# RWKV attention and a SoLU layer on one core: loads from three queues, and turning by DMA instead of by TensorE

## The chip, the cores and the metric

The kernel runs on one core of one Trainium2 chip. The metric is the device time of one execution in microseconds (us). The engines of the core work side by side, each through its own list of instructions in order: PE (TensorE, the matmuls), DVE (VectorE), ACT (ScalarE), POOL (GpSimd) and SP (SyncE, which computes nothing here and issues transfers). Transfers between the main memory and the on-chip memory, and within the latter, are carried out by 16 DMA engines; an engine that issues one goes on while it runs.

## The reference

Two layers follow each other. The first is a linear attention with a decaying state, for 4 batches, 8 heads, 768 steps and a head size of 48:

```python
for t in range(S):
    cur = np.einsum('bhd,bhe->bhde', u[None] * kt, vt)
    y[:, :, t] = np.einsum('bhd,bhde->bhe', rt, state + cur)
    state = wt[:, :, :, None] * state + np.einsum('bhd,bhe->bhde', kt, vt)
```

Its result, 3072 rows (batch and step) of 384 numbers (head and element), goes through the second:

```python
h = x @ w_in                                   # 384 -> 1024
sm = softmax(h);  solu = h * sm
ln = (solu - mean(solu)) / sqrt(var(solu) + 1e-06) * g_ln
out = ln @ w_out                               # 1024 -> 384
```

Inputs and outputs are float32; r, k, v and w are 4.7 MB each, w_in and w_out 1.6 MB each, the result 4.7 MB.

## The kernel before, in words

The sequence is cut into 6 chunks of 128 steps. A **unit** is one chunk of one batch, 128 rows: 24 units, numbered 0 to 23, four (one per batch) to a chunk. A unit needs four loads, the r, k, v and w of its 128 steps for all heads; each is 192 KB, in 1024 pieces of 48 floats (192 bytes).

What is done for a unit is written as short **words**, and ORDER (line 21) is the list of all words in the order in which they are recorded: a letter name, the unit's number, and after a dot an engine (a = ACT, d = DVE, p = POOL, g = POOL's queue) or the PSUM bank that PE writes. Every engine runs its instructions in the order of the words; the class InOrder (line 72, whose call at line 86 records nearly every instruction, so that nearly all of the profile carries line 86) pins it. Engines wait for each other only where data or a buffer demands it. The order was written out ahead; nothing is scheduled afterwards.

The words of a unit, in the order in which its data flows:

- LW, LK, LR, LV: its four loads, all issued by SP before the change. Each lands in one of 7 buffers (NIO) that units take in turn, so unit i+7 loads only after unit i has been read.
- lw: logarithm of w (ACT). cum: two matmuls that sum the logarithms over time (PE). ex: exponential of both (ACT). kp: k and r scaled by them (DVE), 128 x 1024 in bf16, the heads padded to 64.
- krk, krr: k and r turned, so that the head's elements lie on the partitions: four 128 x 128 transposes each on PE. kr: that result copied out of PSUM (ACT or DVE).
- M: eight small matmuls, the scores. m: scores copied out, masked at once (DVE) or afterwards by sel (POOL).
- p, q, qh, dg, dv: the diagonal term with u (POOL and DVE). vb: v in bf16.
- S, et, st: the state after the chunk, in two buffers per batch. Y, y: the attention's result, 128 x 384.
- X, xT: y turned by three transposes on PE, and copied out (ACT or DVE).
- H: the hidden layer, h with the 1024 features on partitions, 24 matmuls. e: exponential (ACT). he: h times it (DVE). ea: the two halves of e added (POOL), in some units. hq: he squared (ACT or DVE).
- Oa, Ob: he times the prepared w_out (eight matmuls of 385 columns). Matmuls of one column in between sum e (or ea) and hq for the normalisation.
- sq, qm, lv, o, out: the variance, its root, the scaled result, and its store.

The weights come in by LI (w_in, three loads of 512 KB) and LO (w_out, two of 768 KB), are cast or scaled by wi, gw, mn, mc and ce. H of the first unit needs all of w_in. The words hot.. are matmuls on zeros that keep TensorE's clock up while it would idle early on.

In the built program a transfer issued by SP waits on one of eight counters taken in turn, so it is issued only when the transfer eight places before it has landed.

Of the kernel before, what the change touches and what calls it, by code (L numbers as in the profile page):

```python
# [8 lines left out]
F32 = mybir.dt.float32  # L9
# [11 lines left out]
ORDER = """  # L21
LW2 LU0 ik0 lw2 hot5.4 cum2.0 LW1 lw1 us0.7 ih0 LW3 lw3 cum3.2 LR2 uc0 ex2 LK2 p2 LV2 vb2.p kp2 hot4.4 krk2.6 krr2
LR1 LK1 cum1.4 LW0 ex1 kp1 kr2.d hot1.0 S2.7 lw0 et2 LV1 vb1.d LW4 st2 p1 q1 hot2.0 krk1.1 krr1 q2 qh2 dg2 LG0
kr1.a M2.4 ex3 hot1.0 M1.6 m1.d dv2 LR0 LK0 p0 q0 cum0.0 ex0 lw4 cum4.6 ex4 kp0 krk0.1 krr0 LR3 gs0.0 gc0 dg1
m2.d Y2.i0 kr0.d LK3 p3 LR4 LV0 vb0.a dg0 dv1 kp3 Y1.i5 hot3.1 krk3.4 krr3 LK4 kp4 M0.2 m0.d krk4.1 y1.a X1.5
krr4 y2.a X2.0 dv0 xT2.d hot1.6 Y0.n7 y0.d kr3.a M3.2 hot1.0 X0.6 S1.4 p4 q3 kr4.a xT1.a xT0.a LI2 LI1 wi1.a
M4.0 m4.a et1 LI0 S0.5 et0 wi0.d m3.d LO1 wi2.p H1.6 e1 gw5.a H2.0 e2 H0.2 LO0 gw2.a q4 qh4 dg4 qh3 dg3 gw4.p
gw7.p LV3 vb3.p dv3 sel4 LW6 e0 gw6.d st1 LV4 vb4.p he1 lw6 dv4 gw1.d LW5 gw0.d gw3.d mn0.4 mc0 ce5.p ce6.p
Y3.i7 ce4.p he2 st0 he0 cum6.0 y3.a ce7.p hot1.5 X3.6 lw5 xT3.a ce3.d LK6 LR6 p6 Y4.n5 LR5 LK5 ce2.d hq0.a ex6
LW7 cum5.2 H3.6 p5 y4.d ex5 ce1.d ce0.d Oa0.5 kp6 krk6.1 krr6 S4.0 hq1.d Oa1.4 kp5 krk5.3 krr5 X4.2 Ob1 e3 he3  # L30
LV5 q6 q5 kr5.d hq2.a et4 st4 M5.6 kr6.a M6.0 xT4.d lw7 cum7.2 hq3.a sq1 m6.a m5.d dg5 vb5.d qm1 dv5 Ob0 ex7 sq0
qm0 S3.7 qh6 LR7 LK7 p7 kp7 et3 lv1 st3 lv0 H4.0 Y5.n6 y5.d LR9 LK8 o1.d e4 krk7.3 krr7 Oa2.2 he4 X5.7 q7 kr7.d
LW9 lw9 o0.a LK9 p9 LW8 lw8 S5.6 et5 cum9.4 ex9 Ob2 sq2 LR8 p8 st5 dg6 kp9 qm2 LV6 xT5.a LV9 vb6.p dv6 sel6
cum8.0 ex8 kp8 hq4.a LV7 LV11 out1 LW10 dg7 vb7.p dv7 Oa3.3 vb9.a lv2 H5.6 e5 M7.4 m7.d he5 q8 krk9.1 LK10 krr9
kr9.a S9.0 et9 Ob3 sq3 st9 q9 qm3 o2.a out0 ea5.p Y6.i5 y6.a LV8 LR10 Y7.n4 y7.d LW11 LW12 krk8.1 M9.6 lw10 lv3
X6.2 xT6.a m9.d o3.a krr8 LV10 out3 out2 kr8.d qh9 dg9 dg8 hq5.d cum10.4 ex10 kp10 S6.0 vb11.d et6 X7.2 xT7.a
st6 p10 vb8.d dv8 dv9 H6.6 e6 he6 H7.2 lw11 e7 he7 M8.4 m8.a Oa5.1 Y9.n0 Ob5 sq5 y9.d cum11.6 ex11 krk10.5 krr10
qm5 kr10.d S7.4 et7 st7 Oa4.3 hq6.d lv5 lw12 o5.a X9.2 sel8 Y8.i0 vb10.p y8.a LK11 LR11 kp11 xT9.d q10 dg10 p11
M10.4 m10.a sel10 S10.1 et10 st10 dv10 S8.0 et8 S11.7 et11 X8.6 xT8.a LK12 LW13 cum12.4 q11 ex12 lw13 st11 st8
Ob4 sq4 qm4 LW14 LR12 kp12 p12 lw14 lv4 o4.a out5 LK13 LV12 LR13 Y10.n2 dg11 y10.d H8.6 e8 krk12.1 krk11.0 krr11  # L40
krr12 kr12.d he8 kr11.a q12 qh12 cum13.4 H9.2 vb12.p S12.1 ex13 p13 q13 ea7.p dg12 kp13 dv11 LW16 LR14 LK14 e9
he9 et12 st12 M12.6 m12.a Oa6.0 X10.5 xT10.a krk13.4 krr13 kr13.a M11.6 m11.d ea8.p dv12 sel12 p14 cum14.2 ex14
q14 out4 Ob6 sq6 hq8.d M13.4 m13.d LV13 hq7.a LW15 lw15 lw16 kp14 vb13.d H10.6 dg13 qm6 LW18 lw18 Y11.n1 y11.d
Oa8.5 LK16 LR15 LR16 LK15 e10 he10 hq9.a krk14.4 Y12.i3 krr14 lv6 qh14 kr14.d p15 ea10.p dv13 LR18 LV14 vb14.p
q15 qh15 LK18 p18 Ob8 sq8 qm8 y12.a S13.2 et13 st13 o6.a lv8 X11.1 xT11.d cum16.6 ex16 X12.3 hq10.d LW19 kp16
Oa9.4 cum15.0 xT12.a Ob9 ex15 kp15 sq9 o8.a dg14 dv14 qm9 M14.2 m14.a sel14 krk16.7 Oa7.6 krr16 kr16.d lv9 o9.d
cum18.0 ex18 kp18 Ob7 LV15 S14.5 et14 st14 krk15.3 krr15 kr15.d LK19 Y13.i2 lw19 cum19.0 krk18.7 p16 q16 vb15.a
S15.4 y13.a sq7 qm7 dg15 X13.5 xT13.d ex19 LR19 kp19 lv7 o7.a q18 krr18 kr18.d H11.2 et15 st15 krk19.5 krr19
kr19.d LW17 lw17 cum17.0 e11 he11 ex17 ea11.p out8 LK17 LR17 p17 kp17 H12.6 e12 he12 hq11.a p19 H13.4 e13 Oa10.3
Y14.n2 M16.0 m16.a dg16 q19 dv15 y14.d ea12.p ea13.p M15.6 m15.d he13 Ob10 sq10 X14.2 out9 Oa11.1 LW20 qm10 lw20  # L50
cum20.6 hq12.d krk17.0 krr17 out6 out7 LV16 vb16.a dv16 xT14.a S16.2 LR20 ex20 LK20 dg18 et16 st16 lv10 o10.a
H14.4 e14 kp20 Ob11 sq11 kr17.d LK23 qm11 lv11 o11.a Oa12.2 krk20.3 krr20 kr20.a he14 sel16 Y16.n7 y16.d Y15.n6
y15.d M19.4 m19.a M18.0 m18.d Ob12 X15.7 xT15.a q17 hq13.d LV19 LW21 LV17 X16.3 xT16.a ea14.p vb19.a M17.4 m17.d
sq12 LK22 out10 qm12 dg17 qh19 vb17.p sel19 p20 hq14.a LW22 LV20 q20 qh20 dv17 M20.0 LV21 m20.d out11 LK21 H15.6
e15 he15 lw22 ea15.p H16.4 LV18 vb18.p dv18 LR21 p21 lw21 Oa14.3 Y17.n1 LR22 LV23 q21 dg19 dv19 Ob14 LR23 p23
p22 e16 he16 lv12 Oa13.0 LW23 o12.a out12 sq14 qm14 hq15.d vb20.a lv14 dg20 dv20 y17.d cum21.6 ex21 Ob13 cum22.4
sq13 ex22 LV22 vb22.p ea16.p o14.d out14 Y18.n2 y18.d Oa15.1 X18.3 qm13 kp22 lv13 xT18.d X17.2 xT17.a kp21 Ob15
sq15 qm15 S18.5 et18 st18 Y19.n4 y19.d lv15 o15.a out15 o13.a krk22.2 S17.3 et17 lw23 H18.6 e18 ea18.p hq16.d
vb21.d st17 Y20.n5 y20.d X19.4 xT19.d krr22 kr22.a H17.0 he18 hq18.d cum23.4 ex23 kp23 Oa16.3 e17 ea17.p he17
krk21.2 krr21 kr21.a H19.6 e19 krk23.5 X20.4 krr23 q22 qh21 vb23.p out13 xT20.a kr23.a he19 Oa18.2 Ob16 sq16  # L60
M21.0 q23 ea19.p qh23 dg22 dv22 m21.a sel21 qm16 lv16 M22.6 hq19.a M23.4 Ob18 sq18 dg21 H20.0 o16.a out16 m22.d
m23.d Oa19.7 Y22.n6 qm18 lv18 hq17.d Ob19 S19.5 dg23 dv23 e20 Oa17.4 y22.d X22.3 he20 et19 st19 xT22.d dv21
Y21.n6 Ob17 y21.d sq19 o18.a sq17 qm17 lv17 Y23.n1 out18 qm19 lv19 X21.0 xT21.d H22.2 o17.a e22 out17 ea20.p
y23.d H21.0 X23.5 xT23.a e21 hq20.d o19.d out19 Oa20.6 he22 hq22.d H23.4 e23 he21 hq21.d Ob20 sq20 qm20 lv20
o20.a out20 ea22.p Oa22.7 ea21.p Oa21.3 he23 hq23.d Ob22 sq22 qm22 lv22 Ob21 sq21 qm21 lv21 o21.d o22.a out22
out21 ea23.p Oa23.2 Ob23 sq23 qm23 lv23 o23.a out23
"""

NIO, NLW, NKP, NWK = 7, 10, 6, 4


class InOrder:


    def __init__(self, tc, engine):
        self.tc, self.engine, self.last = tc, engine, None

    def __getattr__(self, name):
        make = getattr(self.engine, name)

        def call(*args, **kwargs):
            if self.last is None:
                made = make(*args, **kwargs)
            else:
                with self.tc.issue_after(self.last):
                    made = make(*args, **kwargs)  # L86
            self.last = made.ins
            return made

        return call  # L90
# [3 lines left out]
def kernel(  # L94
# [25 lines left out]
    pe, act, dve, pool, sp = (InOrder(tc, e) for e in (nc.tensor, nc.scalar, nc.vector, nc.gpsimd, nc.sync))  # L120
# [34 lines left out]
    g_rows = consts.tile([KF, 128], F32)  # L155

# [57 lines left out]
    qm_t = ring("qm", NWK, [C, 1], F32)  # L214
    lv_t = ring("lv", NWK, [C, 1], F32)
    rs_t = ring("rs", NWK, [C, 1], F32)

    u_bc = consts.tile([C, H, D], BF16)
# [27 lines left out]
    def load_w(i, x):  # L246
        sp.dma_start(out=w_t[i % NIO][:, :, :D], in_=rows_of(w, i))

    def load_k(i, x):
        sp.dma_start(out=kr_t[i % NIO][:, 0, :, :D], in_=rows_of(k, i))  # L250

    def load_r(i, x):
        sp.dma_start(out=kr_t[i % NIO][:, 1, :, :D], in_=rows_of(r, i))

    def load_v(i, x):
        sp.dma_start(out=v_t[i % NIO][:, :, :D], in_=rows_of(v, i))

    def load_u(i, x):
        sp.dma_start(out=u_row, in_=u.rearrange("(o h) d -> o (h d)", o=1))

    def load_g(i, x):
        sp.dma_start(out=g_rows, in_=moe_g_ln.rearrange("(ko ki) -> ko ki", ki=128))

    def load_w_in(j, x):
        sp.dma_start(out=win_f[:, j, :], in_=moe_w_in[j * 128:(j + 1) * 128, :])

    def load_w_out(j, x):
        part = slice(j * KF // 2, (j + 1) * KF // 2)
        sp.dma_start(out=wout_f[:, part, :],
                     in_=moe_w_out.rearrange("(ko ki) d -> ki ko d", ki=128)[:, part, :])  # L270
# [109 lines left out]

    def scores(i, x):
# [86 lines left out]

    def hidden(i, x):
        xT = xT_t[i % NWK]  # L470
        h_ps = live[i]["h_ps"] = bank([128, KF, C], F32, x, "h_ps")
# [4 lines left out]

    def hidden_exp(i, x):
        act.activation(out=e_t[i % NWK], in_=live[i]["h_ps"], func=EXP)
# [7 lines left out]
    def hidden_mul(i, x):  # L486
        dve.tensor_mul(out=he_t[i % NWK], in0=live[i]["h_ps"], in1=e_t[i % NWK])
# [96 lines left out]
```

## Time and profile before

| What | before |
|---|---|
| time, median of 3 runs | 155.79 us (155.73 to 155.89) |
| the profiled execution's span, first to last instruction | 152.4 us |
| busy: PE, DVE, ACT, POOL | 136.4, 131.8, 120.0, 119.0 us |
| TensorE's mean granted clock | 0.975 |
| transfers | 104825 packets, 27.06 MB |

The profile is of one execution. Its span runs from the first instruction to the last; the time of a run also holds what lies around them, here 3.4 us (155.8 - 152.4). Busy times are sums over the span. Matmuls overlap each other, and the ends given for them are modelled, so the distance from one start to the next tells what a matmul costs. The strip in 40 slices shows each engine's busy share in tenths, and under "DMA" that of the 16 DMA engines.

### The profile page before, as it was taken

What the parts mean: (1) busy time and instruction counts of PE and PEld (TensorE: products, weight loads), DVE (VectorE), ACT (ScalarE), POOL (GpSimd) and SP (SyncE); (2) the same over time, 40 slices, a digit from 0 to 9 for tenths busy, and PEclk for the clock granted to TensorE, in tenths of its full rate; (3) what the DMA queues carried; (4) which work ended last, traced back from release to release, by engine and by line L of the source; (5) the groups of instructions that cost most, each with busy time, mean ns of one, the idle gap of its engine ahead of it and who ended that gap; (6) DMA issues with size and microseconds to landing.
All of it is one profiled execution on the core that took longest, in us unless ns stands there. A gap on an engine that the chain in (4) does not pass through costs nothing.

```text
span 152.4 us, 5172 instructions
## 1 busy us (share of the span) xinstructions
PE 136.4 (90%) x2093; PEld 105.5 (69%) x2093; DVE 131.8 (87%) x227; ACT 120.0 (79%) x247; POOL 119.0 (78%) x149
## 2 busy tenths in 40 slices
PE   6777598968999999999998999999799999999970
PEld 1242365936778889779776689887686988889740
DVE  5029968899999999998999999999999999988940
ACT  4526648869888999799998889998988789938661
POOL 7268986799909994899999997799889979973600
PEclk9959969999999999999999999999999999999998
DMA  3999999989979999989897989995998110112023
GB/s 76 218 216 211 217 334 377 254 175 223 216 151 216 220 204 229 206 177 224 194 203 144 228 195 275 199 199 136 241 205 210 63 45 4 44 63 103 4 79 127
DMA packets 104825, 27.06 MB, mean 178 GB/s; under 512 B 100314, under 2 KB 104419, under 8 KB 104803
## 3 DMA queue, kind: packets, MB, share of 16 engines
q1 hardware_dynamic: 104802, 26.75, 77.4%
q8 instruction: 16, 0.26, 0.7%
q14 instruction: 7, 0.05, 0.1%
HBM read 22.03 MB, written 4.72 MB: 176 GB/s over the span
## 4 chain that ended last, share of the span: by engine, by line
PE 53%; DVE 23%; SPq 8%; ACT 6%; issue 3%; DMA 2%; POOL 1%; DVEq 0%; POOLq 0%
PE ps L86 53%; SPq L86 7%; DVE he L86 6%; DVE m L86 4%; DVE kp L86 4%; DVE w L86 3%; DMA kr_in<-in_k_dram 2%; DVE kr L86 1%; DVE hq L86 1%; DVE y L86 1%; DVE st L86 1%; ACT ps L86 1%; ACT o L86 1%; DVE dg L86 1%; ACT win_sb L86 1%
## 5 line engine op out<-in xcount | busy, mean ns | idle before, releaser
L86 PE MATMUL ps<-w,he 128*128 128x385 bf16 x192 | 44.5, 325 | 1.0 <-DVE w L86 0.7
L86 PE MATMUL ps<-xT,win_sb 128*128 128x128 bf16 x576 | 35.5, 219 | 1.1 <-DVE qm L86 0.8
L86 PEld LDWEIGHTS <-win_sb 128*128 128x128 bf16 x576 | 32.8, 98 | 2.2 <-DVE m L86 0.9
L86 PE MATMUL ps<-one_col,hq 128*128 128x1 bf16 x192 | 31.5, 164 | 0.0
L86 DVE TENSOR_TENSOR he<-ps,e 128x1024 bf16<-128x1024 f32 x24 | 29.1, 1214 | 1.6 <-ACT e L86 1.6
L86 DVE TENSOR_TENSOR kp<-ps,kr_in 128x768 bf16<-128x768 f32 x24 | 22.8, 951 | 7.7 <-DMA kr_in<-in_k_dram 4.9
L86 POOL TENSOR_TENSOR p<-kr_in 128x384 bf16<-128x384 f32 x24 | 24.7, 1038 | 4.5 <-DMA kr_in<-in_k_dram 4.2
L86 POOL TENSOR_TENSOR dv<-vb,dg 128x384 bf16<-128x384 bf16 x24 | 21.7, 907 | 7.5 <-DVE qm L86 3.6
L86 ACT ACTIVATE e<-ps 128x1024 bf16<-128x1024 f32 x24 | 24.5, 1021 | 3.1 <-PE ps L86 2.0
L86 POOL TENSOR_TENSOR ea<-e 128x512 bf16<-128x512 bf16 x17 | 20.0, 1181 | 6.4 <-ACT e L86 5.7
L86 POOL TENSOR_TENSOR q<-p,u_bc 128x384 bf16<-128x384 bf16 x24 | 22.2, 931 | 2.4 <-DVE dg L86 1.7
L86 ACT ACTIVATE ps<-ps 128x768 f32<-128x768 f32 x24 | 19.1, 799 | 5.1 <-PE ps L86 4.3
L86 PEld LDWEIGHTS <-kp 128*128 128x128 bf16 x272 | 17.5, 100 | 6.0 <-DVE kp L86 3.2
L86 PEld LDWEIGHTS <-he 128*128 128x128 bf16 x192 | 18.4, 96 | 4.0
L86 PEld LDWEIGHTS <-hq 128*128 128x128 bf16 x192 | 15.4, 96 | 8.3
L86 DVE TENSOR_TENSOR m<-ps,keep 128x1024 bf16<-128x1024 f32 x15 | 18.2, 1216 | 1.2 <-PE ps L86 1.0
L86 PE MATMUL ps<-ident,kp 128*128 128x128 bf16 x192 | 16.5, 227 | 1.6 <-POOL p L86 1.1
L86 DVE TENSOR_TENSOR hq<-he 128x1024 bf16<-128x1024 bf16 x15 | 13.4, 890 | 0.1
L86 ACT COPY kr<-ps 128x1024 bf16<-128x1024 bf16 x11 | 11.1, 1012 | 2.4 <-PE ps L86 2.4
L86 ACT ACTIVATE lw<-w_in 128x384 bf16<-128x384 f32 x23 | 11.7, 523 | 1.3 <-DMA w_in<-in_w_dram 1.3
L86 PEld LDWEIGHTS <-kr 64*128 64x128 bf16 (+1 forms) x272 | 10.2, 95 | 3.1 <-ACT kr L86 0.7
L86 PE MATMUL ps<-inv_col,ea 128*128 128x1 bf16 x68 | 11.2, 165 | 0.0
(90 smaller groups left out, 293.7 us busy)
## 6 DMA issues: line engine op xcount, KB each, us to landing
w_in<-in_w_dram SPq DMA_DIRECT2D x24, 192.0 KB, 3.7
kr_in<-in_r_dram SPq DMA_DIRECT2D x24, 192.0 KB, 3.7
kr_in<-in_k_dram SPq DMA_DIRECT2D x24, 192.0 KB, 3.7
v_in<-in_v_dram SPq DMA_DIRECT2D x24, 192.0 KB, 3.6
out_dram<-o SPq DMA_DIRECT2D x24, 192.0 KB, 2.6
win_f<-in_moe_w_in_dram SPq DMA_DIRECT2D x3, 512.0 KB, 6.4
wout_f<-in_moe_w_out_dram SPq DMA_DIRECT2D x2, 768.0 KB, 9.0
u_row<-in_u_dram SPq DMA_DIRECT2D x1, 1.5 KB
```

Source lines behind the costliest of these rows:

```text
L86: made = make(*args, **kwargs)
```

## The change

- Loads may be issued by SP, by ACT's queue (".a") or by POOL's (".g"): of the 96 loads of units, 44 stay on SP, 37 go to ACT and 15 to POOL; two of the three loads of w_in go to ACT. Stores stay on SP.
- For units 12 to 23 the words krk, krr, kr and X, xT are gone. In their place stand kt and xt: SP issues a transfer that reads kp (or y) in on-chip memory, turns it on the way, and writes the turned tile.
- For seven units (14, 16, 17, 18, 19, 21, 22) h is computed with rows on partitions (six matmuls of 512 columns instead of 24 of 128). The exponential and the square then give their sums over the features as they are computed (ACT's accumulated output), so that the one-column matmuls and ea fall away; he is turned by a third kind of transfer, ht, before Oa.
- The last unit's hidden layer is done in two halves (HA, EA, DA, QA and HB, EB, DB, QB).
- All other squares are ACT's; DVE squares only the last unit's halves. ea is kept in 9 units instead of 17.
- Transfers of SP and ACT are recorded as one sequence in the order of the words; the eight counters are shared by the two.
- The order is new throughout. Loads and attention of more units come ahead of the weights: in the new order 43 loads of units stand ahead of the last load of w_in (20 before).
- Code for a third way to square (g_ps, below) is there, but no unit uses it.

```diff
 ORDER = """
...
+LW0 LW1.a LR0 LU0 LK0.a LV1 LW3.a lw0 LR1 hot10.0 cum0.4 LV3.g LV5.g lw1 cum1.0 ih0 LK1.a ex0 us0.2 ik0 ex1 p0 kp0
...
+Y2.i5 kp7 cum8.1 kp9 krk7.6 LW10 y2.a vb8.a kr6.d q5 gs0.7 p7 dv4 krr7 X2.3 q6 Y3.i4 LO0 LW11 ex8 S7.0 gc0 LV9.g
+LI0.a kr7.d M7.5 wi1.p kp8 M5.1 krk8.7 y3.a X3.4 xT2.d m7.d gw6.a krr8 Y4.i3 M6.5 xT3.d S6.4 kr8.d gw4.a LK10.a
+m5.a LR10.a krk9.1 S8.7 m6.d gw5.a dg5 wi2.p gw7.a et7 lw10 y4.a krr9 wi0.p LW14 st7 kr9.d sel5 LR14.a et8 LR11
+cum10.5 st8 et6 H0.2 LW17 LW12 st6 H1.0 dv5 LK12 vb9.p ex10 LK14.a e0 kp10 dg6 Y5.i4 gw0.p gw2.p gw3.a he0 H3.5 q7
...
+LK18.a hq5.a Oa4.3 X9.4 he7 out2 LR19.a Ob4 dv10 kt13 he6 dg11 xT9.d p15 sq4 X8.6 Y10.n5 S12.7 et12 hq6.a y10.d qm4
+xT8.d st12 Oa5.2 M14.0 p14 M11.4 vb15.p vb13.p lv4 rs4 m11.a m14.d o4.d kt12 Ob5 ea7.p ea6.p sq5 qm5 lw18 LK20 lw19
...
+M18.2 ea12.p m18.d LK21.a e13 Ob10 sq10 qm10 LW23 S15.0 lw21 lv10 Y15.n6 dg17 et15 y15.d rs10 dv17 xt14 p18 H14.2
...
+HA23.0 Ob19 ht21 hq20.a he22 out18 HB23.3 sv21 ht22 sq19 qm19 Oa20.7 EA23 lv19 DA23 rs19 hq21.a sv22 Oa21.4 o19.d
...
-    pe, act, dve, pool, sp = (InOrder(tc, e) for e in (nc.tensor, nc.scalar, nc.vector, nc.gpsimd, nc.sync))
+    pe, act, dve, pool, sp = (InOrder(tc, e, e in (nc.scalar, nc.sync))
+                              for e in (nc.tensor, nc.scalar, nc.vector, nc.gpsimd, nc.sync))
+    queue = {"": sp, "a": act, "g": pool}
...
     def load_w(i, x):
-        sp.dma_start(out=w_t[i % NIO][:, :, :D], in_=rows_of(w, i))
+        queue[x].dma_start(out=w_t[i % NIO][:, :, :D], in_=rows_of(w, i))
...
+    def turned_kr(i, x):
+        sp.dma_start_transpose(out=kr_s[i % NKP], in_=kp_t[i % NKP].rearrange("t a h d -> t (a h d)"))
+
+    def turned_x(i, x):
+        sp.dma_start_transpose(out=xT_t[i % NWK], in_=y_t[i % NWK])
+
+    def turned_he(i, x):
+        sp.dma_start_transpose(out=he_t[i % NWK], in_=ht_t[i % NHT])
...
     def hidden(i, x):
         xT = xT_t[i % NWK]
+        if i in by_rows:
+            h_ps = live[i]["h_ps"] = bank([C, 2, 512], F32, x, "h_ps")
+            for j in range(KM):
+                for n in range(2):
+                    pe.matmul(h_ps[:, n, :], lhsT=xT[:, j, :], rhs=win_sb[:, j, n * 512:(n + 1) * 512],
+                              start=(j == 0), stop=(j == KM - 1))
+            return
...
+            act.activation(out=flat(e_t[i % NWK]), in_=flat(live[i]["h_ps"]), func=EXP, accum_out=be_t[i % NWK])
...
+            dve.tensor_mul(out=ht_t[i % NHT], in0=flat(live[i]["h_ps"]), in1=flat(e_t[i % NWK]))
...
+            act.activation(out=flat(hq), in_=ht_t[i % NHT], func=SQUARE, accum_out=s2_t[i % NWK])
...
+            if i in by_rows:
+                pe.matmul(o_ps[:, :DM + 1], lhsT=he[:, f, :], rhs=w2[:, f, :], start=(f == 0), stop=(f == KF - 1))
+                continue
...
+                pe.matmul(L["g_ps"], lhsT=he[:, f, :], rhs=he[:, f, :], start=(f == 0), stop=(f == KF - 1))
```

## The prediction

> **What bounds the kernel now.** First the strip of 40 slices, for where each engine is full:
>
> ```profile
> PE   6777598968999999999998999999799999999970
> DVE  5029968899999999998999999999999999988940
> ...
> DMA  3999999989979999989897989995998110112023
> GB/s 76 218 216 211 217 334 377 254 175 223 216 151 216 220 204 229 206 177 224 194 203 144 228 195 275 199 199 136 241 205 210 63 45 4 44 63 103 4 79 127
> ```
>
> PE is full from slice 12 (43 us) to the end; the DMA engines are full from slice 2 to 31 (4 to 118 us) and nearly idle after. Then the chain of work that ended last, in order of time, and PE's own waits, longest first:
>
> ```profile
> 43.27 31.86 PE ps L86 x551
> ...
> 110.34 37.23 PE ps L86 x601
> ...
> 148.56 0.58 ACT o L86
> ...
> PE ps L86 <- DVE w L86: 2.1, 3, 0.9
> PE ps L86 <- ACT lw L86: 2.1, 2, 1.4
> ```
>
> No wait of PE is over 1.4 us, and the last 37 us before the closing scalar steps are PE without a gap. So what sets the end is when PE can start in earnest (43 us) and how much work is then left; and the start is set by loads. For the prices, PE's timeline (start, length, instruction: the distance of the starts is the cost) and the transfers between 76 and 87 us, where SP issues loads alone:
>
> ```profile
> 119.83 1.50 PE L86 MATMUL ps<-xT,win_sb 128*128 128x128 bf16 x24
> 121.17 0.33 PE L86 MATMUL ps<-st,kr 128*128 128x96 bf16 x4
> 121.34 0.36 PE L86 MATMUL ps<-vb,m 128*128 128x48 bf16 x8
> 121.55 0.33 PE L86 MATMUL ps<-ident,y 128*128 128x128 bf16 x3
> 121.72 0.39 PE L86 MATMUL ps<-ident,kp 128*128 128x128 bf16 x4
> ...
> 124.56 0.61 PE L86 MATMUL ps<-ident,kp 128*128 128x128 bf16 x8
> 125.01 1.50 PE L86 MATMUL ps<-xT,win_sb 128*128 128x128 bf16 x24
> ```
>
> ```profile
> DMA packets 10922, 2.08 MB, mean 189 GB/s; under 512 B 10921, under 2 KB 10921, under 8 KB 10921
> ...
> q1 hardware_dynamic: 10921, 2.07, 96.5%
> ```
>
> 96.5% of 16 engines for 11 us over 10921 packets is 15.6 ns a packet; a load, 64 packets on each engine, is 1.0 us of all 16. The five weight loads (3.15 MB) at the 377 GB/s of slice 7 are 8.4 us. From 126 to 146 us only stores run: share 0.14, 52 GB/s, so 0.53 us a store. 96 x 0.995 + 8.4 + 24 x 0.53 = 116.6 us; the page's 77.4% of 152.4 is 118.0.
>
> **PE.** From the starts: 24 hidden matmuls 1.34 us, eight transposes 0.45, three 0.17, half an output with ea 0.81 (123.75 to 124.56), one matmul of 385 columns 0.165. Turning by DMA takes 12 x (0.45 + 0.17) = 7.4 us off PE. A unit by rows has eight matmuls of 385 columns, 1.32 instead of 1.62; its six of 512 columns are, by their columns, 6 x 0.22 = 1.32 instead of 1.34: 7 x 0.32 = 2.2 us. Four more warm-ups (0.86) lie in the early idle time. Summed so over all words PE goes from 125.4 to 116.5 us. As a check: before, the words from cum of unit 7 (43.6 us) on sum to 100.4 us and PE ended at 147.6, 104.0 later; I scale what is left by 1.036.
>
> **The other engines**, by the rows of the costliest groups (busy, mean ns of one), of which three:
>
> ```profile
> L86 DVE TENSOR_TENSOR hq<-he 128x1024 bf16<-128x1024 bf16 x15 | 13.4, 890 | 0.1
> ...
> L86 ACT COPY kr<-ps 128x1024 bf16<-128x1024 bf16 x11 | 11.1, 1012 | 2.4 <-PE ps L86 2.4
> ...
> L86 ACT ACTIVATE hq<-he 128x1024 bf16<-128x1024 bf16 x9 | 9.5, 1055 | 0.5 <-DVE he L86 0.5
> ...
> SPq L86 <- ACT o L86: 22.2, 9, 5.1
> ```
>
> The last line is SP's longest wait, used below. DVE loses 15 squares (13.4), six vb (3.8), weights (3.7), three kr (2.0), gains ten o (6.1), three m (3.7), one y (0.6), 1.4 for sums over unhalved q, 1.1 for halves: 131.8 to 121.8. ACT gains 14 squares (14.8), vb (2.0), w (2.4), seven small squares (1.2), loses nine kr (9.1), twelve xT (5.8), ten o (5.8), three m, one y and a cast (4.5): 120.0 to 115.2. The sums over features have no row: not below nothing, as no element is dropped, and at most one rs (0.2) each, 14 x 0.2 = 2.8; I take 0. ACT's queue also issues 39 loads. SP's issue of a lone load takes 0.37 to 0.43 us, one right behind another 0.87 (median of k's): 14 to 34 us; ACT's stand three us apart, nearest to the lone ones, so 17, and ACT 132. POOL loses eight ea, three sel, seven qh, gains two vb and two casts (-13.6, to 105.4) and issues 15 loads, each between SP's lone 0.37 and its longest, 4.1; nearest to neither, as POOL shows none: 1.0 taken, sum 120. None passes the 150 us of the paths below. The last unit in halves: before, PE has no gap at the end, so I give it 0 (between -0.7, half a hidden layer overlapped, and +0.9 for one more exponential and product in line).
>
> **The transfers.** A turn of kp or he reads 1024 rows of 256 bytes. The nearest row is a load of 1024 packets of 192 bytes; 64 more bytes at 377 GB/s over 16 engines are 2.7 ns, so 18.3 ns a packet, 1.16 us. xt, 384 rows: 0.44. Low end: 256 KB at 377 GB/s, 0.70. High end: nothing overlaps and each holds the engines for a load's median flight, 3.7. Taken: 1.16, and 19 x 1.16 + 12 x 0.44 = 27 us more on engines that are full until 118 us. Every turn waits on SP for its source (kp from DVE for kt, y for xt, the product for ht), and behind it on SP stand loads of units 18 to 23 and the stores; eight places on, the shared counters make ACT wait too, with its exponentials behind (LR22 on ACT waits for kt16's place, LK23 for kt17's).
>
> **The sum.** Transfers in word order, first packet at 2.2 us:
> - To LI0, the last of w_in: 43 loads, 8.4 of weights: 53.4 us (before: 20 loads; DVE's cast began at 25.2). One cast on POOL, 1.0, then H of unit 0, from which PE has 94.7 x 1.036 = 98.1 left: PE ends at 152.5. Half of the nine POOL loads ahead may be overtaken (4.5): 148.0.
> - To kt12: 75 loads, 8.4, four stores, three turns: 90.8; from M12 PE has 62.0 x 1.036 = 64.2 left: 155.0. xt14 (90 loads, ten stores, seven kt, three xt: 114.9; 40.2 left): 155.1. Seven others are in flight, so up to 7 us can be overtaken; half is 3.5: 151.5.
>
> The later one holds: PE ends at 151.5 instead of 147.6. Behind PE's end the old trace has 4.8 us of scalar steps and store, and 3.4 lie around the span: 159.7, say **159.5 us** against the 155.79 median. What goes out of PE (8.9 us) is lost in the start (H of unit 0 some 25 us later) and to the fuller DMA engines. This case's own range: all seven overtaken 156.2, none 163.3.
>
> **Rivals.**
> - *Faster: no DMA idle time.* In the strip of 76 to 87 us slices of 250 to 260 GB/s stand beside some of 9 to 75, and SP waits 22.2 us for ACT's o ahead of stores. Loads on ACT's and POOL's queues don't stand behind stores. At 225 GB/s a load is 0.87: LI0 at 48.0, PE's end 147.1, with half the overtaking (3.9) 143.2; kt12 at 81.5, 145.7, less 3.0 is 142.7. Time 151.4. It decides once PE ends before 147.6, from loads of 0.94 on. Against it: full slices already stand at 9, and at the start, where only loads run, the window from 4 to 24 us has share 1.05.
>  The Trainium skill ("DMA: Bandwidth & Descriptors", "Issuing engines are not separate DMA queues") says that transfers of all issuers run on the same 16 engines and interleave, and that several issuers save only the time to issue; by it a load stays at 1.0 and this rival gains only what is idle. The trace agrees so far as one queue fills all 16.
> - *Slower: ACT becomes the bound.* With 0.87 an issue, ACT's sum is 115.2 + 34 = 149.1; ACT idles 6.1 us of the last 12.4 and about 3 of the first 10, which gives 158.3, time 161.7, up to 165 with waits on counters. For: ACT was busy 9.97 of 10 us from 70 to 80. Against: its issues stand apart.
> - *Much slower: dear turns.* At twice the load's packet time, 2.3 us, xt23 (all loads, 18 stores, 17 large turns and 12 small ones) comes at 165.1 and PE ends 8.3 later: time 181.6; at 3.7 us each, 211. For: no row shows a turn. Against: same rows, same bytes.
>  By the Trainium skill ("VectorE: DVE Perf Modes", "The three transpose paths") a block of 128 x 128 takes 1309 ns by DMA and 390 on TensorE. An estimate by it, 188 blocks one after another, is 246 us, beyond 250 us in all; TensorE's here cost 56 ns, so that such single figures hold mostly fixed time.
> - *The gain and the loss cancel:* PE's end within 0.3 us of 147.6.
>
> **Chances.** Main case 0.42, idle time gone 0.32, ACT 0.13, dear turns 0.09, cancelling 0.04. 0.2% (0.3 us) is about what a measurement of this kernel can tell from no change. Faster: 0.32 and 0.01 of the main case's rim: 0.33; same 0.04; slower 0.63. The range goes from 149 (a good part of the faster case, about 0.1 below) to 170 (ACT's case inside, dear turns out).
>
> **What would show it.** Right: H of unit 0 starting at 48 to 54 us; DMA at 9 until about 130 us; PE with gaps before M12, H14 or H16 whose releaser is a DMA; PE's transposes down to 96 + 36. Wrong: a load's packets clearly under 15 ns or slices above 240 GB/s throughout (faster), ACT-issued loads of 0.8 us or more (ACT), turns landing after more than 6 us (dear), or PE without waits and H of unit 0 before 46 us.

## The result, and the profile after

The changed kernel takes **160.71 us** (median of 4 runs, 159.66 to 161.41) against 155.76 us (4 runs) of the kernel before: a ratio of 1.034, 95% interval 1.028 to 1.040. It is slower, as forecast (159.5 us). Its profiled execution took 161.41 us with a span of 159.7. Some executions of a kernel take over 1.5% longer than its fastest one; the times and ratios of the experiments leave these out.

The strip of the changed kernel in 40 slices of 4 us (busy tenths; GB/s moved):

```profile
PE   6868548979496899999839999968997799999970
...
PEclk9999985799969789999995999999999789999999
DMA  5999999999999569499997998999899967388432
GB/s 106 290 275 256 290 290 256 258 401 380 280 231 200 108 143 206 134 216 186 224 258 222 189 129 192 261 201 190 195 172 201 244 137 181 99 130 221 123 140 101
```

Three things are to be seen. The loads ahead of the weights move at 256 to 290 GB/s, where the kernel before had 211 to 218. The DMA engines are full through slice 31 (128 us; before 118), but for slices 13, 14, 16 and 21 (52, 56, 64 and 84 us). And PE, which was busy 9 tenths and more in nearly every slice from 43 us on, now has holes: slices 10, 12, 20, 26 and 30 to 31 (40, 48, 80, 104 and 120 us). In or after all but that at 104 us the granted clock drops to 0.5 to 0.7.

Where PE waited, from its timeline after the first H (start, length, instruction; in brackets the idle time just before it and what ended it):

```profile
42.49 4.44 PE L86 MATMUL ps<-xT,win_sb 128*128 128x128 bf16 x48 [2.28 <-POOL win_sb L86]
...
52.52 0.33 PE L86 MATMUL ps<-st,kr 128*128 128x96 bf16 x4 [1.91 <-DVE kr L86]
...
84.05 0.40 PE L86 MATMUL ps<-kr 64*128 64x128 bf16 x8 [2.65 <-DMA kr<-kp]
84.38 2.73 PE L86 MATMUL ps<-xT,win_sb 128*128 128x128 bf16 x24
...
87.93 1.50 PE L86 MATMUL ps<-xT,win_sb 128*128 128x128 bf16 x24
...
106.45 1.51 PE L86 MATMUL ps<-xT,win_sb 128*128 128x128 bf16 x24 [1.28 <-DMA xT<-y]
...
111.19 1.47 PE L86 MATMUL ps<-win_sb,xT 128*128 128x512 bf16 x5 [0.37 <-DMA xT<-y]
...
124.94 0.39 PE L86 MATMUL ps<-win_sb,xT 128*128 128x512 bf16 x1 [0.97 <-DMA xT<-y]
```

The lines with a wait are H of unit 0 (42.5 us), Y of unit 6, whose bank still held kr of unit 10, and then M12, H13, H14 and H16: from M12 on it is a turned tile that comes last, but for one wait of 0.97 us on ACT's et at 123.3 us. The two lines without a wait are the same 24 hidden matmuls: right behind the hole of 2.65 us they took 2.73 us, 3.5 us later 1.50. The chain of work that ended last says the same; before, its DMA share was 2% and PE's 53%:

```profile
DMA 33%; PE 26%; ACT 13%; POOL 9%; issue 7%; DVE 7%; SPq 3%; ACTq 0%; POOLq 0%
```

Its pieces in order of time (start, length, what) show which transfers:

```profile
75.67 8.34 DMA kr<-kp
...
84.05 3.07 PE ps L86 x32
...
106.39 4.75 DMA xT<-y
...
111.63 7.01 PE ps L86 x100
...
119.38 5.52 DMA xT<-y
```

The turn in front of M12 took 8.3 us from issue to landing, 3.9 of which SP spent on issuing it. The medians, from the page's DMA issues (how many, us to landing):

```profile
kr<-kp SPq DMA_TRANSPOSE x12, 5.2
xT<-y SPq DMA_TRANSPOSE x12, 2.8
he<-win_f SPq DMA_TRANSPOSE x7, 2.8
```

### The profile page after: what moved, and what is told of

Its sections match the earlier page's. It is cut to its first block, busy times and chain, and to the rows that moved or that the text cites. A ratio compares the mean times of both kernels' runs of the same rounds, so it can differ in the third digit from the quotient of the medians.

```text
span 159.7 us, 4569 instructions
## 1 busy us (share of the span) xinstructions
PE 133.9 (84%) x1750; PEld 96.4 (60%) x1758; DVE 124.5 (78%) x215; ACT 116.3 (73%) x255; POOL 115.1 (72%) x150
## 3 DMA queue, kind: packets, MB, share of 16 engines
q10 hardware_dynamic: 38768, 8.33, 27.6%
## 4 chain that ended last, share of the span: by engine, by line
DMA 33%; PE 26%; ACT 13%; POOL 9%; issue 7%; DVE 7%; SPq 3%; ACTq 0%; POOLq 0%
PE ps L86 26%; DMA xT<-y 6%; DMA w_in<-in_w_dram 6%; DMA kr<-kp 5%; DMA win_f<-in_moe_w_in_dram 5%; DMA kr_in<-in_k_dram 4%; ACT hq L86 3%; DMA v_in<-in_v_dram 3%; SPq L86 3%; ACT e L86 3%; DMA kr_in<-in_r_dram 3%; POOL q L86 2%; DVE kp L86 2%; POOL ea L86 2%; POOL p L86 1%
## 5 line engine op out<-in xcount | busy, mean ns | idle before, releaser
L86 ACT ACTIVATE e<-ps 128x1024 bf16<-128x1024 f32 (+1 forms) x25 | 24.6, 986 | 11.9 <-PE ps L86 10.6
L86 PE MATMUL ps<-xT,win_sb 128*128 128x128 bf16 x408 | 29.0, 236 | 3.6 <-POOL win_sb L86 2.3
L86 PEld LDWEIGHTS <-win_sb 128*128 128x128 bf16 x408 | 26.6, 106 | 5.2 <-POOL win_sb L86 2.7
L86 PE MATMUL ps<-one_col,hq 128*128 128x1 bf16 x136 | 22.3, 164 | 0.6 <-ACT hq L86 0.5
L86 DVE TENSOR_TENSOR he<-ps,e 128x1024 bf16<-128x1024 f32 (+1 forms) x18 | 20.7, 1157 | 1.6 <-ACT e L86 1.6
L86 ACT ACTIVATE hq<-he 128x1024 bf16<-128x1024 bf16 x16 | 16.6, 1052 | 2.5 <-issue 1.3
L86 POOL DMA_DIRECT2D v_in<-in_v_dram x15 | 14.1, 938 | 0.0
L86 POOL TENSOR_TENSOR ea<-e 128x512 bf16<-128x512 bf16 x9 | 10.3, 1154 | 4.5 <-ACT sq L86 3.0
L86 PE MATMUL ps<-kr 64*128 64x128 bf16 x192 | 9.8, 229 | 4.1 <-DMA kr<-kp 2.6
L86 DVE TENSOR_TENSOR y<-ps,dv 128x384 bf16<-128x384 f32 x18 | 9.8, 552 | 3.6 <-POOL q L86 2.2
```

## The experiments

Twelve kernels ran. Ratios are to the kernel before on the same chip, each with its 95% interval. "PE's end" is the start of PE's last matmul in the profile (before 147.4, changed 154.7), "first H" the start of H of the first unit (before 26.1, changed 42.5). In the four runs below that keep the changed kernel up to its first H, this lies at 40.9 to 42.6 us; so a difference of less than 2 us in it says nothing.

### One queue for all loads

```diff
-LW0 LW1.a LR0 LU0 LK0.a LV1 LW3.a ... LV3.g LV5.g
+LW0 LW1 LR0 LU0 LK0 LV1 LW3 ... LV3 LV5
```

> The new kernel with all loads issued by SP again, in the same order of words; turns stay on SP. If several queues let the DMA engines carry more (278 to 290 GB/s in the first 25 us of the new kernel against 211 to 218 before), H of unit 0 comes at 50 to 54 us instead of 42.5 and the time is 168 to 175. If the queues change nothing but the issuing (my prediction's premise), H of unit 0 stays near 43 and the time at 160 to 162; if issuing on ACT and POOL is itself the cost, it falls below 158.

Measured: 175.3 us (two executions), ratio 1.132 (1.125 to 1.140), just above the 168 to 175 us forecast. First H at **54.2 us**, PE's end 168.0. The strip of this kernel:

```profile
DMA  5999999998999899939999999999689996747552
GB/s 112 212 207 192 202 205 220 211 213 211 375 272 264 160 224 183 202 92 230 205 205 163 220 176 182 235 172 216 136 187 154 251 194 135 195 110 177 135 169 91
```

The full engines of one queue move 192 to 220 GB/s ahead of the weights, those of three 256 to 290. The shares say the same: 1.05 with one queue (4 to 36 us, 207 GB/s), 1.23 with three (4 to 32 us, 274 GB/s). The start moves by 11.7 us of the 13.3 by which PE's end moves. So packets of several queues do pass beside each other here, and within the new order the three queues are worth some 15 us (1.132 against 1.034).

### POOL's loads on ACT

```diff
-LV3.g LV5.g ... LV2.g ... LV16.a
+LV3.a LV5.a ... LV2.a ... LV16.a
```

> The changed kernel with its 15 loads on POOL's queue issued by ACT instead, at the same words. Theory (POOL's issuing, 15 x 0.94 = 14 us, stands in front of POOL's own work, on which the attention's dv and the masks wait): first H near 42, POOL's waits shrink, 156 to 159 us. Rival (the third queue's packets pass beside the others, and POOL isn't what is waited for): ACT gets 15 x 0.43 = 6.5 us more, the head's slices fall below 260 GB/s, 162 to 168 us.

Measured: 162.05 us, ratio 1.048 (1.042 to 1.054), against 1.034 (1.028 to 1.040) of the changed kernel. First H at 47.0 us, slices of 235 to 262 GB/s from 4 to 32 us, at a share of 1.24. The rival holds, at its lower edge: POOL's 14 us of issuing are not what is waited for, and the third queue brings the first H from 47.0 to 42.5 us. One queue, two, three: 54.2, 47.0, 42.5. Whether the last step is the third queue or the larger packets in which POOL's loads move (3072 bytes instead of 192) was not tried.

### Nothing turned by DMA

The changed kernel with the words of old for k, r and y, and the seven units no longer by rows (in place of each turn, for instance unit 14's):

```diff
-kt14
+krk14.0 krr14 kr14.d
-xt14
+X14.7 xT14.d
-sv14 ... ht14
```

> The new order and the loads from three queues, but nothing is turned by DMA: kt, xt and ht are taken out, krk, krr, kr (copied by DVE), X and xT (DVE) stand in their places, and the seven units by rows go the old way. PE gets 9.6 us of work back; behind the first H (42.5 us in the new kernel) it has 104.3 x 1.036 = 108 us left. If late turns make the 14 us of PE's gaps (my theory now), PE runs without them: its end at 150 to 152, time 158 to 160. If the new order leaves PE waiting for ACT, DVE and POOL whatever turns (rival), the gaps stay and the time is 166 to 172.

Measured: 171.68 us, ratio 1.108 (1.103 to 1.113). First H at 42.0, PE's end 163.4. The rival holds: no turn is left, and the kernel is 11 us slower still. PE's longest waits in it:

```profile
PE ps L87 <- DVE kp L87: 5.6, 9, 0.9
PE ps L87 <- DVE kr L87: 4.5, 5, 2.2
PE ps L87 <- ACT lw L87: 3.5, 2, 1.8
```

None is on a transfer, the chain of work that ended last has none behind 45.1 us, and the engines have room (share 0.10 to 0.61 from 80 us on). I put the words of old into the changed order by hand, at the places of the turns and on banks that were free there; an order written for them would do better. So 11 us bounds from above what turning is worth. The queues' rows give the price of the turns, first of the changed kernel, then of this one (packets, MB, share of 16 engines):

```profile
q1 hardware_dynamic: 75490, 21.64, 60.9%
q10 hardware_dynamic: 38768, 8.33, 27.6%
q0 software_dynamic: 960, 2.95, 6.7%
```

```profile
q1 hardware_dynamic: 50434, 15.48, 37.0%
q10 hardware_dynamic: 38768, 8.33, 23.1%
q0 software_dynamic: 960, 2.95, 5.5%
```

95.2% of 159.7 us against 65.6% of 169.0: 152.0 - 110.9 = 41 us of 16 engines for 25056 packets, 26.3 ns a packet (some of it is what other packets lost beside them).

### Only k and r not turned by DMA

```diff
-kt14
+krk14.0 krr14 kr14.d
```

> Of the new kernel only the turns of k and r (kt, 12 of 256 KB) go back to PE, copied by DVE; xt and ht stay. PE gets 5.4 us more. If the large kt, which land in 5.2 us (median) while loads run, are the late ones: PE's end near 42.5 + (94.7 + 5.4) x 1.036 + 3 to 5 of gaps = 149 to 151, time 157 to 160. If the order is what leaves gaps: 165 to 168.

Measured: 165.41 us, ratio 1.070 (1.064 to 1.076). The rival again. By the queues' rows the engines have 78.2% of 163.0 us, 127.5, so by the same reckoning twelve kt hold 24.5 us of them, 2.0 each.

### The early half of those twelve

The same for units 12 to 17 alone, those whose turns fall where the DMA engines are full. This run came after the one with small loads, which is shown next and on which its theory rests.

```diff
-kt14 ... kt13 ... kt12 ... kt15 ... kt16 ... kt17
+krk14.0 krr14 kr14.d ...
```

> The changed kernel, with k and r of units 12 to 17 turned by TensorE and copied by VectorE again (as all twelve were in the run without kt); units 18 to 23 stay with DMA. Theory (with small loads the changed kernel took 152.3 instead of 160.7 us, so full DMA engines cost it 8 us; the six early turns, some 2 us of 16 engines each, lie just there and hold up the loads): without them 157 to 160 us. Rival (the 7 us of PE, 4 of VectorE that the six units bring back weigh more, as in the run without any kt, which took 4.7 us more than the changed kernel: 12 x 0.39): 162 to 164 us.

Measured: 161.75 us, ratio 1.046 (1.041 to 1.050). Neither number was hit squarely, but the theory falls: taking the six early turns away does not help, it costs 1.2%, a third of what all twelve cost (3.6%). In this order, with words of old put back by hand, a turn is worth its place even in the full stretch. (The 7 us of PE and 4 of VectorE in the forecast are too much: six units are 6 x 0.45 = 2.7 us of PE by the prediction's price, and VectorE's busy time rose by 2.8.)

### Loads without their bytes

heads(i) is the first head of eight for units 12 to 23 and all eight else; k, r and v are cut in the same way.

```diff
-queue[x].dma_start(out=w_t[i % NIO][:, :, :D], in_=rows_of(w, i))
+queue[x].dma_start(out=w_t[i % NIO][:, heads(i), :D], in_=rows_of(w, i)[:, heads(i), :])
```

> The changed kernel, but each of the 48 loads of units 12 to 23 brings one head of eight (128 packets instead of 1024); issues, waits and words stay, the other seven heads keep the numbers of an earlier unit, so that the output is not the reference's. This takes 48 x 7/8 x 0.995 = 42 us of 16 DMA engines away, nearly all of it after the first H. Theory (PE's gaps after the first H come from hand-offs between engines in this order of the words): the gaps stay, first H near 42, time 156 to 161 us. Rival (the gaps come from crowded DMA engines: late loads, late turns): PE runs on from the first H as it did before, 42.5 + 98.1 x 1.036 = 144.1, plus 8.2, so 151 to 154 us, and no wait of PE on a turned tile over 0.5 us.

Measured: 152.02 us, ratio 0.983 (0.976 to 0.990). First H at 42.6, PE's end 145.4. The rival holds, and with it my reading of the runs without turns and without kt falls: the waits on transfers were not just the face of gaps that the order has anyway. PE's share of the chain that ended last goes from 26% to 58%, DMA's from 33% to 18%. (The rival's 144.1 scales by 1.036 twice; once gives 42.5 + 98.1 = 140.6 and a time of 148.8. That the time fell into its 151 to 154 is luck.) Windows of 10 us, the changed kernel first, then this run (after the window: sum, busy us of PE, PEld, DVE, ACT and POOL, PE's clock, DMA share, GB/s):

```profile
50.00:60.00 10.00, 8.09 (x105) 6.29 (x104) 8.04 (x13) 6.43 (x12) 7.82 (x10) 0.83 0.70 143
80.00:90.00 10.00, 7.35 (x102) 6.29 (x97) 6.44 (x9) 5.57 (x14) 7.28 (x9) 0.83 1.01 225
120.00:130.00 10.00, 8.00 (x88) 4.68 (x86) 6.49 (x11) 5.88 (x15) 7.64 (x10) 0.83 1.02 216
```

```profile
50.00:60.00 10.00, 8.09 (x105) 6.21 (x103) 8.19 (x13) 6.43 (x11) 7.97 (x10) 0.83 0.18 39
80.00:90.00 10.00, 10.00 (x174) 8.48 (x173) 9.71 (x15) 9.69 (x19) 9.96 (x14) 1.00 0.53 108
120.00:130.00 10.00, 8.95 (x104) 5.38 (x100) 8.80 (x13) 8.73 (x25) 7.18 (x10) 1.00 0.58 144
```

The hole from 50 to 60 us stays: it is a hand-off (Y of unit 6 waits 1.9 us until DVE has copied kr of unit 10 out of its bank), not a transfer. The hole from 80 to 90 goes, and half of that from 120 to 130. PE's end moves by 9.3 us. One piece was not as the rival had it: a wait of 1.05 us on a turned y at 124.4 us stays.

### The same in the old order

The kernel with small loads, and the old list of words in it.

```diff
-LW0 LW1.a LR0 LU0 LK0.a LV1 LW3.a lw0 LR1 hot10.0 cum0.4 LV3.g ...
+LW2 LU0 ik0 lw2 hot5.4 cum2.0 LW1 lw1 us0.7 ih0 LW3 lw3 cum3.2 ...
```

> The old order and queue, with the loads of units 12 to 23 cut to one head of eight as in the changed kernel's run with small loads (the output is not the reference's). A control for that run, which went from 160.7 to 152.3 us. Theory (the old order has enough room that full DMA engines cost PE nothing after 43 us; the new one hasn't): at most 1% faster than before, 153.5 to 155.5 us. Rival (small loads make any order faster, through fewer waits of SP or less contention): 3 to 5% faster, 147 to 150 us.

Measured: 154.64 us, ratio 1.002 (0.999 to 1.005). The control holds: in the old order the packets of the late loads cost nothing. With the DMA engines relieved the new order is the faster one (0.983 against 1.002); with them full it is the slower.

### Loads from three queues in the old order

```diff
-LW2 LU0 ik0 lw2 hot5.4 cum2.0 LW1 lw1 ... LV0 ... LK4 ... LI1 ... LI0
+LW2 LK2.a LR2 LW1.a LU0 LW3.a LK1.a LR1 ik0 LV2.g LV1.g ... LV0.g ... LK4.a ... LI1.a ... LI0.a
```

> The old order, nothing turned by DMA, nothing by rows; only the first loads are spread: seven v loads to POOL, k of units 0 to 4, w of 1 and 3 and two of w_in to ACT. If several queues carry more, the old kernel's H of unit 1 comes at 20 to 23 us instead of 26, PE is full from 39 to 41 instead of 43, and the time is 151.5 to 154. If not, 155 to 157; if POOL's 6.5 us of issuing hurts, over 157.

Measured: 162.84 us, ratio 1.051 (1.046 to 1.057), a miss. The packets did run faster (275 to 281 GB/s in the second and third slice), but first H came at 35.8 us. PE's timeline shows where it stood:

```profile
30.84 0.61 PE L87 MATMUL ps<-ident,kp 128*128 128x128 bf16 x4 [6.61 <-DVE kp L87]
```

k of unit 4 stood on ACT's list and was issued at 18.0 us, right behind a load of w_in; POOL's p waited 8.2 us for it. So spreading loads changes in which order they arrive, and this run measures my spread, not the queues.

### The same with less moved

```diff
-LW2 LU0 ik0 lw2 hot5.4 cum2.0 LW1 lw1 us0.7 ih0 ... LR2 ... LV2 ... LR1 LK1 ... LV1 ... LK0 ... LV0 ... LV3
+LW2 LU0 LW1.a LR2.a ik0 lw2 hot5.4 cum2.0 lw1 us0.7 ih0 LV2.g LR1.g LV1.g LK0.g LV0.g LV3.g ... LK2 LK1
```

> The old order, with 8 of the first 20 loads off SP: LW1 and LR2 on ACT at the very start, LR1, LK0 and the v of units 0 to 3 on POOL after its first word. SP's loads keep their places except LK1, so nothing waits behind an overtaken load. Theory (packets of several queues pass beside each other: 278 to 290 GB/s in the new head instead of 211 to 218): the first loads and w_in land 3 to 5 us earlier, the first H comes at 21 to 24 instead of 26, and PE, full from 43 us to its end, ends 1 to 3 us earlier: 152.5 to 155 us. Rival (the start is set by hand-offs among the first units and not by the rate of the loads, or the spread changes their order for the worse): 155.5 to 159 us.

Measured: 155.32 us, ratio 1.006 (1.003 to 1.010). The two windows from 10 to 30 us move 285 GB/s each (before 216 and 335), and first H is at 27.6 us (before 26.1). The time lies between the two forecasts, and the theory falls: this spread gains nothing. The chain of work that ended last shows what stands in the way:

```profile
4.83 1.07 POOL v_in L87
...
8.54 1.75 POOL v_in L87 x2
...
10.30 0.55 POOL p L87
```

POOL issues its six loads from 4.8 to 10.3 us, ahead of its own work. Its first p starts at 10.3 us (before 7.8), and the chain stays on POOL until 20.4 us; no transfer is on it. So it is the cost of issuing on POOL that this run shows. What faster loads alone would be worth to the old start it leaves open.

### Late turns in the old order

Twelve turns: kt in units 21 to 23, xt in 16, 18, 19 and 20, and units 16 to 20 by rows; shown for one unit of each.

```diff
-krk21.2 krr21 kr21.a
+kt21
-X18.3 ... xT18.d
+xt18
-ea18.p ... hq18.d
+ht18 ... hq18.a ... sv18
```

> The old order and the old queue (SP alone), with the new ways only near the end, when the DMA engines are idle: k, r of units 21 to 23 and y of units 16, 18, 19, 20 turned by DMA, units 16 to 20 by rows with he turned by DMA and their sums accumulated by ACT. By the terms of the prediction PE loses 3 x 0.45 + 4 x 0.17 + 5 x 0.32 = 3.6 us. Theory (turning pays where the engines are free and PE is the bound; what cost time was the order): PE ends 2 to 3.6 us earlier, 152 to 154 us. Rival (a turn lands 2.8 to 5.2 us after its issue and each one opens a gap of PE): 155.5 to 159 us.

Measured: 166.00 us, ratio 1.075 (1.070 to 1.080), worse than both forecasts. SP's timeline at the place, and the windows around it:

```profile
95.85 3.10 SPq L86 DMA_DIRECT2D kr_in<-in_k_dram  x2
106.65 1.28 SPq L86 DMA_TRANSPOSE xT<-y  x1
107.99 0.56 SPq L86 DMA_DIRECT2D v_in<-in_v_dram  x1
```

```profile
100.00:110.00 10.00, 10.00 (x178) 8.31 (x176) 9.90 (x15) 7.72 (x17) 7.69 (x8) 1.00 0.20 41
110.00:120.00 10.00, 6.85 (x68) 4.14 (x66) 5.70 (x10) 6.78 (x16) 5.87 (x7) 0.93 1.03 221
```

SP stood from 98.95 to 106.65 us for the y of a turn, with loads behind it; the DMA engines fell to a share of 0.20, and PE ran dry 10 us later.

### Late turns behind the last load

As in the last run, with every turn behind the last load: nine turns (kt in 21 to 23, xt in 18 to 20, by rows 17, 19 and 20).

```diff
-xt16 ... ht16 ... ht18
+X16.3 xT16.a ... ea16.p ... ea18.p
```

> As the earlier run with late turns in the old order, but every turn is issued after the last load (v of unit 22): k, r of units 21 to 23 and y of units 18 to 20 turned by DMA, units 17, 19 and 20 by rows. Behind a turn on SP stand only stores. By the prediction's terms PE loses 3 x 0.45 + 3 x 0.17 + 3 x 0.32 = 2.8 us. Theory (166.0 us came from SP, which stood at 98.95 to 106.65 us for the y of a turn, with the loads of units 18 to 23 behind it): no such stop, DMA share back to 0.9 from 100 to 110 us, PE ends 2 to 3 us earlier, 151.5 to 153.5 us against about 154.5 to 155.8 of before. Rival (each turn's own 3 to 5 us of flight opens gaps of PE, wherever SP stands): 155.5 to 160 us, with waits of PE on xT, kr or he above 1 us each.

Measured: one execution at 154.91 us and five from 157.82 to 159.84 (before 154.48); they scatter too far for a ratio with an interval. None reaches the theory's 151.5 to 153.5. SP's stop is gone: the share from 100 to 110 us is 0.90 again, as the theory had it. But PE, whose own work is 2.8 us less, waits in the profiled execution, which is one of the five (157.82 us):

```profile
122.02 1.51 PE L86 MATMUL ps<-xT,win_sb 128*128 128x128 bf16 x24 [1.95 <-DMA xT<-y]
130.49 0.40 PE L86 MATMUL ps<-kr 64*128 64x128 bf16 x8 [0.73 <-DVE win_f L86]
131.47 0.40 PE L86 MATMUL ps<-kr 64*128 64x128 bf16 x8 [0.58 <-DMA kr<-kp]
135.79 0.83 PE L86 MATMUL ps<-w,he 128*128 128x385 bf16 x4 [1.71 <-DMA he<-win_f]
```

Three turned tiles come 0.6 to 2.0 us late though the last load was issued at 115.1 us (the median flights are 2.4 us for y, 3.2 for k and r, 3.5 for he). So of the 11.5 us that late turns had cost, 6 to 11 go with SP's stop and three turns fewer. Whether these waits are what sets the five apart from the fastest is not shown, since that one has no profile.

### Of those, only k and r

```diff
-krk21.2 krr21 kr21.a
+kt21
```

> The old order and the old queue; only k and r of units 21 to 23 are turned by DMA, after the last load. Takes 3 x 0.45 = 1.35 us off PE and three copies off ACT. Theory: each word that goes from PE's list shortens its end, 153.2 to 154.5 us (ratio 0.988 to 0.996); the share of the gain of the three kinds of turn shows against the run with all three. Rival (the score matmuls wait for the turned tile): ratio 1.00 to 1.02.

Measured: 156.2 us (six executions), ratio 1.010 (1.006 to 1.014): the rival. By the prediction's price three turns take 1.35 us off PE, and one of them makes PE wait 1.22 us at 131.35. No version that moves all the bytes was faster than the kernel before.

## Why the prediction was right or wrong, point by point

**The sign and the place were right.** It named M12, H14 and H16 as the places where a turned tile would come last, and DMA engines full until about 130 us. The profile has all three waits, and a strip that is full, but for four slices, until 128 us. H14 started at 111.19 us where the sum had xt14 at 114.9 less 3.5, 111.4. The runs with small loads show the cause: about 8 us of the time (ratio 1.034 to 0.983) hang on the packets of the late loads in the new order, and none in the old. M12 started at 84.05 where the sum had 90.8 less half of 7, 87.3.

**The step that failed is the first term of the sum: "To LI0 ... 53.4 us", and with it the price of 1.0 us a load whatever the queue.** It is right for one queue (first H at 54.2 us in that run) and wrong for three (42.5, outside the 48 to 54 us that were to show the prediction right). At the 274 GB/s of 4 to 32 us a load of 192 KB is 0.72 us; with that the term is 2.2 + 43 x 0.72 + 8.4 = 41.6, and LI0 landed at 41.3. The rival without idle time had 48.0 for it and was nearer. I had argued from one queue's share of 1.05 that the engines were full; a full engine of one queue still took packets of another: the share of the changed kernel from 10 to 20 us is 1.24. The Trainium skill ("DMA: Bandwidth & Descriptors", "Issuing engines are not separate DMA queues") has several issuers save only the time of issuing; by it the start would not have moved. Here the runs with one and two queues, all of whose loads move in packets of 192 bytes, differ by 7 us in the first H, and a third queue brings 4.5 more, so the measurement decides against that reading for such loads.

**Why the earlier start did not make it faster.** PE had 98.1 us left at first H by the sum, which would have put its end at 140.6. It ended at 154.7. Of the 14.1 us between, 9.3 go when the late loads carry an eighth of their bytes; the other 4.8 stay, among them the hole of 1.9 us at 52 us, a hand-off. The prediction's rule that the later of several landings sets the end held in so far as the start did not set it: start and end are not one sum.

**The turns were mis-sized, and this hid the first mistake.** 1.16 us for a large turn was taken; kt cost 2.0 us each, and all turns 41 us instead of 27. In the sum, their packets (26.3 ns against 18.3 assumed) would give back the 12 us that the start had gained, together with engines not full from 50 to 70 us (share 0.70 and 0.78); no run shows how much each gave back. That the landing of xt14 came out to 0.2 us is thus luck in part. Nor was it a place in the line of transfers that set it. Two lines of DVE's timeline show what did:

```profile
104.94 0.96 DVE L86 TENSOR_TENSOR kp<-ps,kr_in 128x768 bf16<-128x768 f32 x1 [1.04 <-DMA kr_in<-in_r_dram]
105.82 0.55 DVE L86 TENSOR_TENSOR y<-ps,dv 128x384 bf16<-128x384 f32 x1
```

The y of unit 14 stood on DVE behind kp of unit 22, which waited 1.04 us for a load of r. SP issued xt14 right behind it, at 106.39 us, and its own flight was 4.75 us. The prediction knew that a turn waits for its source and gave that no term.

The rival of dear turns had nearly the price of kt (2.3 us; that is twice the turn assumed, while twice a load's packets would be 2.0) but not its time, 181.6, since it took one queue's start along. Its sign, landings after more than 6 us, was met by single turns (8.3 at most), not by the median (5.2). The Trainium skill's figure of 1309 ns a block ("VectorE: DVE Perf Modes", "The three transpose paths") is no sum of blocks here: eight blocks of he landed after 2.8 us, 0.35 us a block.

**After H14** the sum had 40.2 us to PE's end and the trace has 43.5: two more waits, 0.97 us each, at 123.3 (ACT's et) and 124.9 (H16), and a clock of 0.83 from 120 to 130 us. PE's end was 3.2 us later than forecast (154.7, not 151.5); behind it came 5.0 us as forecast (4.8), and around the span 1.7 instead of 3.4 in this execution, as in most later executions of the kernel before. That the time came within 1.2 us of the forecast is luck to that extent.

**ACT was not the bound.** Its loads took 0.37 to 0.44 us to issue (medians of the kinds), as taken, and its work 116.3 us (115.2). **POOL** took 0.94 us for each load (1.0), and 115.1 us in all (120). DVE had 124.5 us of work (121.8). The accumulated sums, taken at 0, cost ACT an instruction of their own, the bound of 0.2 us each; from the costliest groups:

```profile
L86 ACT ACTIVATION_READ_ACCUMULATOR e<-ps 128x1 f32 x7 | 1.4, 196 | 0.0
L86 ACT ACTIVATION_READ_ACCUMULATOR hq<-win_f 128x1 f32 x7 | 1.3, 191 | 0.0
```

**What stays open:** how much of the 9.3 us is late loads and how much late turns behind them, since cutting the loads speeds up both (the median flight of kt fell from 5.2 to 3.8 us); and what a planner that knew the turns' flight would make of the old order. Neither was tried.

## What to carry to other kernels

Moving work from a full PE to DMA engines is not paid for by room on these engines: three turns behind the last load took 1.35 us of work off PE and made the kernel 1.0% slower. Count the engines' load where the work lands, in time, and not over the whole span, and set the flight of each turn (2.3 to 8.3 us here) against the time that its reader can wait; in an order written without it this makes new gaps. The wait for its source also blocks the queue that issues it (7.7 us of SP in one run here), so no load should stand behind it. And more queues are worth trying where loads of small packets set the start, but they change the order of arrival, and a faster start is worth only what the next transfer in line lets through.

## What the runs showed of the hardware

- Loads in packets of 192 bytes: one queue moved 192 to 220 GB/s on engines that were full, two 235 to 262; three, with POOL's loads in larger packets, 256 to 290. The engines' share was 1.05 with one queue, 1.24 and 1.23 with two and three. In the middle of the kernel, with turns among them, three queues moved no more than one (174 to 225 GB/s in the windows from 70 to 130 us; before, 194 to 218 from 70 to 110).
- POOL's loads moved in 960 packets in all, for 15 loads of 192 KB: 3072 bytes a packet.
- A turn holds SP's queue for 1.2 to 1.4 us of issuing (median; 3.9 at most among kt), a lone load 0.43.
- In the 10 us around holes of PE of 1.91 and 2.65 us, and around two of 0.97 us, the granted clock was 0.83 on the mean (50 to 60, 80 to 90 and 120 to 130 us); around one of 1.28 us (100 to 110) it was 1.00.
